# Eight groups of four feature tiles of the first layer by seven block products, with Silu gates behind the last exponential

## The chip, the cores and the metric

The kernel runs on one core of a Trainium2 chip. The metric is the device time of one execution in microseconds (us), taken as the median of several runs. TensorE (PE in the profile) multiplies matrices, PEld is its weight load, VectorE (DVE), ScalarE (ACT) and GpSimd (POOL) work on elements, and SyncE (SP) issues most transfers.

## The reference

Attention with routing by clusters, and then a two-layer network with Silu. A query sees the keys that have its cluster.

```python
q_assign = argmax(q_n @ c_n.T); k_assign = argmax(k_n @ c_n.T)      # 16 clusters a head
scores = where(q_assign == k_assign, q @ k.T / sqrt(64), -1e9)
attn = softmax(scores) @ v              # 4 batches, 8 heads, 768 tokens, 64 a head
x = attn.transpose(0, 2, 1, 3).reshape(3072, 512)
h = x @ w_in                            # 512 x 2048
out = (h * sigmoid(h)) @ w_out          # 2048 x 512
```

## The kernel before

The work is cut by batch `b` (0 to 3) and half `c` of a batch's 768 tokens (`HALF` = 384), written (b, c) below.

**Attention.** There are 192 score units: for a head, a half of the queries and two key tiles, `qk_mm` (L354) makes two matmuls of 384 columns and `exp` (L359) one exponential of 768 elements. `pv` (L371) multiplies by the values, with a column of twos for the sum of the weights, so `norm` (L381, L383) gives half of the attention output. It is transposed into `xt`, by a transfer or on TensorE (`xn_t`, L393, for the last).

**First layer.** For each of 16 feature tiles `fb` of 128, `unit_a_rows` (L421) makes four matmuls of 384 columns into a PSUM bank; what comes out is h/2. `tanh` (L441, ScalarE) and `gate` (L444, VectorE) form (tanh(h/2) + 1) * h/2, which is Silu(h), in f16 in the tile `gt`. When all scores have been issued, the two double banks of the scores (tag "st") are free, and `unit_a2` (L467, L468) takes two feature tiles at once there; the code calls these places `halls`.

**Second layer.** Single token tiles go through `part_b` (L480). Pairs of token tiles go through the class `Pair` (L561), which multiplies 2x2 blocks with seven products instead of eight. Its left operands are sums of four blocks (`sums`, L544, on VectorE). Sum 1 and 2 have tiles of their own ("sg"); sum 3 and 4 overwrite rows of `gt` that earlier products read, and so wait for these. Its right operands are sums of weights made once (`tw_piece`, L514).

**The order.** Every instruction's place in its engine's queue is chosen while the program is built, by a planner at the end of the kernel. It holds a clock and a list of ready pieces per engine, with an assumed duration for each piece (a feature tile 0.655 us on TensorE, a gate 0.52 us on VectorE), and issues what is ready, by rank. `options` lists what TensorE may do next: scores when they are due by a pace (`PACE`, `LEAST`, `GAIN`), then waiting pieces, the first layer from the queue `qa`, the second from `qb`. Four single PSUM banks (`bank`, `done`) go around between attention, first and second layer. `unit_piece` takes a feature tile from `qa`; `NU` is the number of score units, so `unit == NU` means that the last scores have been issued. `new_pair` sets up a pair and says which sum waits for what.

Tiles of staging space are reused by tag: "ab0" to "ab11" hold transposed keys and queries, "raw" and "hl" their loads.

Of the kernel before, what the change touches and what calls it, by code (L numbers as in the profile page):

```python
# [34 lines left out]
def kernel(  # L35
# [10 lines left out]
    nc = tc.nc  # L46
# [385 lines left out]
    def unit_a_end(b, c, fb, ph):  # L432
        if (b, c) not in gts:
            gts[b, c] = mp.tile([128, NFB, HALF], f16, name="gt", bufs=2)
        gt = gts[b, c]
        unit_a_rows(ph, b, c, fb, [NR - 1])

        tn = mp.tile([128, HALF], f32, name="tn", bufs=4)

        def tanh():  # L440
            nc.scalar.activation(out=tn, in_=ph[:, 0:HALF], func=AF.Tanh, bias=0.0, scale=1.0)  # L441

        def gate():
            nc.vector.scalar_tensor_tensor(out=gt[:, fb, :], in0=tn, scalar=1.0, in1=ph[:, 0:HALF], op0=ALU.add, op1=ALU.mult)  # L444
            done(ph)

        def act():
            tanh()
            gate()

        act.tanh, act.gate = tanh, gate
        return act

    def unit_a2(b, c, fb):
        if (b, c) not in gts:
            gts[b, c] = mp.tile([128, NFB, HALF], f16, name="gt", bufs=2)
# [4 lines left out]
        tn = mp.tile([128, 2, HALF], f32, name="tn2", tag=f"ab{fb // 2 % 2}", bufs=1)  # L461

        def act():
            act.tanh()
            act.gate()

        act.tanh = lambda: nc.scalar.activation(out=tn, in_=ph[:, :, 0:HALF], func=AF.Tanh, bias=0.0, scale=1.0)  # L467
        act.gate = lambda: nc.vector.scalar_tensor_tensor(  # L468
            out=gt[:, fb : fb + 2, :], in0=tn, scalar=1.0, in1=ph[:, :, 0:HALF], op0=ALU.add, op1=ALU.mult
        )  # L470
        return act
# [58 lines left out]
    class Pair:  # L530

        def __init__(self, kind, b, r1, r2, j2, sgs, last=False):
            self.last = last
            self.kind, self.b, self.j2, self.sgs, self.r1, self.r2 = kind, b, j2, sgs, r1, r2
            self.s1 = self.s2 = None

        def sums(self, k):
            if k == 1:
                self.s1, self.s2 = (mp.tile([128, HK, 128], f16, name="sg", tag=x, bufs=1) for x in self.sgs)
            s1, s2, a11, a12, a21, a22 = self.s1, self.s2, self.r1(0), self.r1(1), self.r2(0), self.r2(1)  # L540
            o, x, y, op = (
                (s1, a21, a22, ALU.add), (s2, s1, a11, ALU.subtract), (a21, a11, a21, ALU.subtract), (a12, a12, s2, ALU.subtract)
            )[k - 1]
            nc.vector.tensor_tensor(out=o, in0=x, in1=y, op=op)  # L544

        def product(self, k):
            if k == 1:
                self.A = bank("po")
                self.B = bank("po3") if self.last else self.A[:, HD:DM]
            if k == 2:  # L550
                self.Y = bank("po2")
            up = k in (3, 5)
            o = (self.Y if k == 2 else self.B if up else self.A)[:, 0:HD]
            l = self.s1 if k == 5 else self.s2 if k == 6 else self.r1(k > 1) if k < 4 else self.r2(k == 4)
            begins = (1, 2, 5) if self.last else (1, 2)
            for f in range(HK):
                if k < 4:
                    x = wout_s[:, f if k == 1 else HK + f, HD * up : HD * up + HD]
                else:
                    x = tw({4: 3, 5: 0, 6: 2, 7: 1}[k], f)[:, 0, :]  # L560
                nc.tensor.matmul(  # L561
                    o, l[:, f, :], x, start=(f == 0 and k in begins), stop=(f == HK - 1), skip_group_check=True
                )
# [39 lines left out]
        def c21_last(self):  # L603
            nc.scalar.activation(out=self.ot2[:, 0:HD], in_=self.A[:, 0:HD], func=AF.Copy, bias=0.0, scale=1.0)
            nc.scalar.dma_start(self.rows()[:, 0, :], self.ot2[:, 0:HD])

    def w_load(n, after=None):
        if after is not None:
# [259 lines left out]
    def chain(job, b):  # L868
# [23 lines left out]
        def landed(t):  # L892
            i = int(job.name[1:])
            turn_at[i] = t
            if i in after_turn:
                after_turn.pop(i)(t)
            turning(t + ROOM[b - 1])
# [138 lines left out]
    for b, c in kinds:  # L1036
# [3 lines left out]
        elif cross:  # L1040
            kinds[b, c] = ["x", 1, 2] if c else [0, 1]

    def room(key):
# [11 lines left out]
    def norm_piece(n, t):  # L1055
        b, c, i = n // 8, n // 4 % 2, n // 8 * H + 2 * (n % 4)

        def ready(t):
            nonlocal released
            if n % 4 == 3:  # L1060
                released += 1
                x_at[b, c] = t
                qa.extend((b, c, fb) for fb in range(NFB))

        def after(t):
            if by_dma(n):
# [20 lines left out]
    def new_pair(b, c, kind):  # L1087
# [3 lines left out]
        r_ = room(key)  # L1091
        if kind == "x":
            r2 = (lambda h: cps[b][h]) if b in cps else tokens(b, 0, NM - 1)
            pairs[key] = Pair(r_, b, tokens(b, 1, 0), r2, NM - 1, SG[r_])
        else:
            pairs[key] = Pair(r_, b, tokens(b, c, t + 1), tokens(b, c, t), c * NM + t, SG[r_], key == LAST)
        watch.setdefault((b, c), []).append((key, "12" if kind == "p" else "1"))
        pr = pairs[key]

# [2 lines left out]

        when(key, ("lo2", "hi2", "turn"), sum_(1, 0.0))
        when(key, ("s1", "lo1"), sum_(2, 0.0))
        when(key, ("s2", "s1", "lo1"), sum_(3, 0.5))
        when(key, ("s2", "hi1", "p2"), sum_(4, 0.5))
        if not users[r_] or "over" in at[users[r_][-1]]:
            tell(key, "turn", 0.0)
        users[r_].append(key)
        def over(t):  # L1110
# [19 lines left out]
    if 0 in CROSS:  # L1130
        kept(0, 0, 1.0)

    def unit_piece(two=False):
        b, c, fb = qa.pop(0)
        if two:
            qa.pop(0)
            halls.pop(0)
        act = (unit_a2 if two else unit_a)(b, c, fb)

        def gated(t):  # L1140
# [4 lines left out]
            for h, name in enumerate(("lo", "hi")):  # L1145
                need = [gate_at.get((b, c, x)) for x in range(h * HK, h * HK + HK)]
                if h == fb // HK and None not in need:
                    for key, rows in watch.get((b, c), ()):
                        for x in rows:
                            tell(key, name + x, max(need))  # L1150
                    if c == 0 and b in CROSS:
                        kept(b, h, t)

        def then(t):
            add("ACT", t + 0.2, 0.8 if two else 0.42, act.tanh, lambda t: add("DVE", t + 0.1, 0.92 if two else 0.52, act.gate, gated))
            if fb == 0 and kinds[b, c][0] != 0:
                for kind in kinds[b, c]:
                    if kind in ("p", "x"):
                        new_pair(b, c, kind)
                    else:  # L1160
                        qb.extend((b, c, kind, n) for n in range(4))
            elif fb == NFB - (2 if two else 1) and kinds[b, c][0] == 0:
                qb.extend((b, c, t_, n) for t_ in kinds[b, c] for n in range(4))

        return then

    def sent(t):
        clock["SP"] = max(clock["SP"], t) + 0.6
# [57 lines left out]
    def options(t):  # L1226
# [3 lines left out]
        if unit < NU and unit - 2 in exp_at and 6 * pv_next > unit - LEAD:  # L1230
            i, c, m = units[unit]
            jn = {qc[i, c][0].name, kt[i, 2 * m][0].name}
            if all(j in code_at for j in jn):
                r = max([exp_at[unit - 2]] + [code_at[j] for j in jn])

                x = unit // 24
                stock = 0.655 * len(qa) + 0.868 * len(qb) + sum(works[released:x])
                for hb in {q[:2] for q in qa}:
                    if kinds[hb][0] == 0 or hb + (0,) in qa:
# [5 lines left out]
        if unit == NU and here and halls and len(qa) > 1 and qa[0][2] % 2 == 0 and qa[0][:2] in x_at:  # L1245
# [20 lines left out]
    def tensor_piece(o):  # L1266
        nonlocal unit, pv_next, turn, scored
        rank, r, length, what = o
        if what == "qk":
            u = unit  # L1270
            unit += 1

            def then(t):
                add("ACT", t + 0.2, 0.75, lambda: exp(u), lambda t: exp_at.__setitem__(u, t), 0.2)

            run("PE", r, length, lambda: qk_mm(u), then)
            scored = max(clock["PE"] - 0.325, scored + 0.8)
# [3 lines left out]
        elif what == "pv":  # L1281
            n = pv_next
            pv_next += 1
            run("PE", r, length, lambda: pv(n // 8 * H + 2 * (n % 4), n // 4 % 2), lambda t: (pv_at.__setitem__(n, t), norm_piece(n, t), [f(t) for f in after_pv.pop(n, [])]))
        elif what in ("a", "aa") or isinstance(what, tuple):
# [21 lines left out]
    while True:  # L1307
# [14 lines left out]
        else:  # L1322
            lanes[e].remove(piece)
            run(e, piece[0], *piece[2:])
    assert not qa and not qb and not later
# [1 line left out]
_INS = ['q', 'k', 'v', 'centroids', 'moe_w_in', 'moe_w_out']  # L1327
_OUTS = [((3072, 512), 'float32')]
# [25 lines left out]
```

## Time and profile before

| | us |
|---|---|
| median of 3 runs | 300.08 |
| the runs | 297.98, 333.51, 300.08 |
| span of the profiled execution | 297.1 |
| TensorE busy | 288.0 (97% of the span) |
| VectorE busy | 219.7 (74%) |
| ScalarE busy | 221.7 (75%) |
| GpSimd busy | 72.3 (24%) |

The profile is of one execution of its own; its span goes from the first to the last instruction, and a run's time lies somewhat above a span. Rows of the groups read: line, engine, operation, output <- inputs, shapes, count | busy us, mean ns of one | idle time of the engine just before, and what ended it. Matmuls overlap in the profile, so the mean of one is its latency and not its issue rate. In the chain of waits each step goes back to what released it; a piece of the chain has a start and a length, and pieces on one engine that touch give its issue rate. A table by stretches has, for each engine, busy time and (x) instructions, then TensorE's granted clock, the share of the DMA engines and GB/s.

### The profile page before, as it was taken

The page shows a single profiled execution, that of the slowest core. Times are in us where ns is not written, and L with a number is a line of the kernel's source. Part 1 is how long each engine was busy: PE and PEld are TensorE (multiplying, and loading weights), DVE is VectorE, ACT ScalarE, POOL GpSimd, SP SyncE. Part 2 cuts the span into 40 slices and gives each one's busy share as a digit, 9 for nine tenths or more (in the row PEclk, how much of TensorE's full clock was granted, in tenths as well). Part 3 has the DMA queues.
Part 4 walks back from the last instruction along what each step waited for, and adds up shares of the span by engine and source line. Part 5 has one row for each costly group of instructions (what it writes and reads, how often), then busy time and mean ns, then how long its engine had stood idle before and what let it go on. Part 6 is the DMA issues. An engine that isn't in the chain of part 4 may idle for free.

```text
span 297.1 us, 8186 instructions
## 1 busy us (share of the span) xinstructions
PE 288.0 (97%) x3273; PEld 203.4 (68%) x3273; DVE 219.7 (74%) x459; ACT 221.7 (75%) x365; POOL 72.3 (24%) x133
## 2 busy tenths in 40 slices
PE   7899799999999999999999999999999999999995
PEld 3786666566766566667766776678767786767783
DVE  5998559586897799997797766997664553569743
ACT  5899689765896579988579668997798879845410
POOL 2889510001031023544232560243200000000000
PEclk9999999999999999999999999999999999999999
DMA  6689999999866599999877979785220020110113
GB/s 208 206 244 204 158 257 228 170 235 185 242 128 174 133 214 227 209 223 196 232 175 144 196 215 226 170 126 119 74 57 17 13 86 15 49 38 0 35 38 141
DMA packets 77220, 44.61 MB, mean 150 GB/s; under 512 B 56288, under 2 KB 73088, under 8 KB 77184
## 3 DMA queue, kind: packets, MB, share of 16 engines
q1 hardware_dynamic: 71952, 35.55, 51.7%
q0 software_dynamic: 4800, 8.13, 15.0%
q8 instruction: 25, 0.41, 0.6%
q10 hardware_dynamic: 432, 0.43, 0.4%
q14 instruction: 11, 0.09, 0.1%
HBM read 27.30 MB, written 6.29 MB: 113 GB/s over the span
## 4 chain that ended last, share of the span: by engine, by line
PE 85%; DMA 7%; POOL 2%; DVE 2%; issue 1%; ACT 1%; SPq 0%; POOLq 0%; DVEq 0%; ACTq 0%
PE ph L421 28%; PE pS L354 18%; PE po L561 16%; PE pO L371 10%; PE po L480 9%; DMA raw<-in_q_dram 3%; PE psN L180 3%; DMA ab<-cd 3%; DMA ab<-cdt 1%; POOL hl L125 1%; DVE hl L132 1%; DVE ab L166 1%; POOL vt L295 1%; POOL win_s L613 0%; PE px L393 0%
## 5 line engine op out<-in xcount | busy, mean ns | idle before, releaser
L359 ACT ACTIVATE P<-pS 128x768 f16<-128x768 f32 x192 | 156.9, 826 | 36.9 <-PE pS L354 36.0
L421 PE MATMUL ph<-xt,win_s 128*128 128x384 f16 x512 | 97.6, 326 | 0.0
L354 PE MATMUL pS<-ab 128*128 128x384 f16 x384 | 93.2, 326 | 2.2 <-DMA ab<-cd 1.5
L444 DVE SCALAR_TENSOR_TENSOR gt<-tn,ph 128x384 f16<-128x384 f32 x110 | 58.7, 550 | 21.0 <-ACT tn L441 20.4
L421 PEld LDWEIGHTS <-win_s 128*128 128x128 f16 x512 | 49.3, 98 | 31.1
L441 ACT ACTIVATE tn<-ph 128x384 f32<-128x384 f32 x110 | 55.1, 514 | 3.3 <-PE ph L421 2.4
L354 PEld LDWEIGHTS <-ab 128*128 128x128 f16 x384 | 34.5, 98 | 20.8 <-issue 2.5
L371 PEld LDWEIGHTS <-P 128*128 128x128 f16 x1152 | 39.7, 97 | 5.0 <-DVE ab L166 0.9
L371 PE MATMUL pO<-vt,P 128*128 128x65 f16 x1152 | 41.2, 193 | 0.3 <-DVE ab L166 0.3
L132 DVE SCALAR_TENSOR_TENSOR hl<-raw,hl 128x768 f16<-128x768 f32 (+3 forms) x35 | 32.8, 939 | 1.2 <-POOL hl L125 0.5
L561 PEld LDWEIGHTS <-gt 128*128 128x128 f16 x304 | 29.3, 98 | 5.9 <-DVE gt L544 0.4
L480 PE MATMUL po<-wout_s,gt 128*128 128x512 f16 x128 | 32.5, 379 | 0.0
L295 POOL CAST vt<-vn 128x384 f16<-128x384 f32 x32 | 18.8, 598 | 56.2 <-DMA vn<-in_v_dram 40.7
L561 PE MATMUL po<-wout_s,gt 128*128 128x256 f16 x192 | 24.4, 273 | 0.0
L224 POOL TENSOR_SCALAR od<-od 128x96 f16<-128x96 f16 x16 | 9.3, 580 | 53.3 <-DVE od L217 53.2
L381 DVE RECIPROCAL zr<-pO 128x6 f32<-128x6 f32 x32 | 6.2, 193 | 18.9 <-PE pO L371 18.8
L180 PEld LDWEIGHTS <-ab 128*128 128x128 f16 x458 | 17.3, 97 | 4.0 <-DVE ab L166 0.3
L480 PEld LDWEIGHTS <-gt 128*128 128x128 f16 x128 | 12.0, 98 | 10.6
L383 DVE TENSOR_TENSOR xn<-pO,zr 128x384 f16<-128x384 f32 x32 | 17.8, 557 | 1.1
L180 PE MATMUL psN<-stk,ab 128*128 128x32 f16 (+1 forms) x458 | 18.6, 188 | 0.0
L561 PE MATMUL po<-tw,sg 128*128 128x256 f16 x128 | 16.3, 273 | 0.0
L192 DVE TENSOR_REDUCE L<-psN 128x192 f32<-128x384 f32 (+1 forms) x27 | 14.8, 549 | 1.9 <-PE psN L180 1.7
(101 smaller groups left out, 259.0 us busy)
## 6 DMA issues: line engine op xcount, KB each, us to landing
raw<-in_k_dram SPq DMA_DIRECT2D x31, 192.0 KB, 4.0
out_dram<-ot SPq DMA_DIRECT2D x23, 256.0 KB, 2.4
raw<-in_q_dram SPq DMA_DIRECT2D x24, 192.0 KB, 3.9
vn<-in_v_dram SPq DMA_DIRECT2D x16, 192.0 KB, 4.2
vn<-in_v_dram POOLq DMA_DIRECT2D x16, 192.0 KB, 4.3
win_s<-in_moe_w_in_dram POOLq DMA_DIRECT2D x8, 256.0 KB, 6.2
wout_s<-in_moe_w_out_dram POOLq DMA_DIRECT2D x4, 512.0 KB, 18.8
raw<-in_q_dram SPq DMA_DIRECT2D x2, 384.0 KB, 4.2
```

Source lines behind the costliest of these rows:

```text
L132: nc.vector.scalar_tensor_tensor(out=hl[:, s, 1, :], in0=raws[job.name][:, s, :], scalar=QS, in1=hl[:, s, 0, :], op0=ALU.mult, op1=ALU.sub ...
L180: nc.tensor.matmul(L[:, n % g, :, n // g], ab[:, i, :], stk[:, job.groups[i // 3][0], x : x + w], start=(x == 0), stop=(x + w == 2 * HC),)
L295: nc.gpsimd.tensor_copy(vt[:, :, 0:D], vns.pop(i))
L354: nc.tensor.matmul(pS[:, e, 0:HALF], abs_[kj.name][:, kn, :], rhs, start=True, stop=True)
L359: nc.scalar.activation(out=P, in_=pst.pop(u)[:, :, 0:HALF], func=AF.Exp, bias=0.0, scale=ESC)
L371: nc.tensor.matmul(o[:, (2 * t + h) * VW : (2 * t + h + 1) * VW], Ps[i + h, c, j // 2][:, j % 2, ts(t, 128)], vtb[(i + h) % 13][:, j, 0:VW ...
L383: nc.vector.tensor_tensor(out=xn, in0=ov[:, :, 0:D], in1=zr.unsqueeze(2).to_broadcast([128, 2 * NM, D]), op=ALU.mult)
L421: nc.tensor.matmul(ph[:, 0:HALF], win_s[:, r, ts(fb, 128)], xts[b, c][:, r, :], start=(r == 0), stop=(r == NR - 1))
L441: nc.scalar.activation(out=tn, in_=ph[:, 0:HALF], func=AF.Tanh, bias=0.0, scale=1.0)
L444: nc.vector.scalar_tensor_tensor(out=gt[:, fb, :], in0=tn, scalar=1.0, in1=ph[:, 0:HALF], op0=ALU.add, op1=ALU.mult)
L480: nc.tensor.matmul(po, gts[b, c][:, fc, ts(t, 128)], wout_s[:, fc, :], start=(fc == 0), stop=(fc == NFB - 1))
L561: nc.tensor.matmul(o, l[:, f, :], x, start=(f == 0 and k in begins), stop=(f == HK - 1), skip_group_check=True)
```

## The change

Three things are changed.

**Groups of four feature tiles by seven block products.** Two groups of (2, 1) and three each of (3, 0) and (3, 1) are listed in `QUADS`; the other feature tiles go one by one as before, in the order of `ORDERS` (an entry from 100 on is a group). In a group the 512 inputs, the four feature tiles and the 384 tokens are each cut in two, and the seven products of a group (class `Quad`) are four matmuls of 192 columns each. The token sums (`x_sum`, 12 VectorE instructions) and the weight sums (`t_piece`, 16 instructions on VectorE or GpSimd) are formed in staging tiles. Two copies out of PSUM and four additions per group put the products together; four activations of 384 elements and their gates follow, on VectorE or, with two instructions, on GpSimd. The planner runs at most two groups at a time before the last scores, and four after that.

**Silu.** Behind the last exponential a table load for Silu is issued, and from then on first-layer results go through one Silu activation with scale 2, straight into `gt`; no gate follows.

**Own tiles.** For the last two pairs of the second layer, sums 3 and 4 have tiles of their own, and wait for no product. `tn2` moves to other tags, and from score unit 155 on the planner uses other numbers for pace and rank.

```diff
 def tanh():
+    if silu_on:
+        nc.scalar.activation(out=gt[:, fb, :], in_=ph[:, 0:HALF], func=AF.Silu, bias=0.0, scale=2.0)
+        done(ph)
+        act.gate = None
+        return
     nc.scalar.activation(out=tn, in_=ph[:, 0:HALF], func=AF.Tanh, bias=0.0, scale=1.0)
...
 def sums(self, k):
     if k == 1:
-        self.s1, self.s2 = (mp.tile([128, HK, 128], f16, name="sg", tag=x, bufs=1) for x in self.sgs)
+        self.s = [mp.tile([128, HK, 128], f16, name="sg", tag=x, bufs=1) for x in self.sgs]
+        if len(self.s) == 2:
+            self.s += [self.r2(0), self.r1(1)]
...
+QUADS = {(2, 1): (2, 3), (3, 0): (1, 2, 3), (3, 1): (1, 2, 3)}
+ORDERS = {(2, 1): [4, 0, 1, 6, 103, 3, 2, 7, 102, 5], (3, 0): [102, 103, 1, 101, 2, 3, 0], (3, 1): [0, 101, 102, 1, 3, 103, 2]}
+HT = HALF // 2
...
+def t_piece(s, r, e, v):
+    TV[0] = v
+    a, b_, op = (
+        (wblk(2 + r, 1), wblk(r, 1), ALU.subtract), (t_at_(0, r), wblk(r, 0), ALU.add),
+        (wblk(2 + r, 0), t_at_(1, r), ALU.subtract), (wblk(r, 1), wblk(r, 0), ALU.subtract),
+    )[s]
+    (nc.gpsimd if e == "P" else nc.vector).tensor_tensor(out=t_at_(s, r), in0=a, in1=b_, op=op)
...
+    a, b_, op = (
+        (a21, a22, ALU.add), (z[:, 0], a11, ALU.subtract), (a11, a21, ALU.subtract), (a12, z[:, 1], ALU.subtract),
+    )[k - 1]
+    nc.vector.tensor_tensor(out=z[:, k - 1], in0=a, in1=b_, op=op)
...
+            def gate(eng):
+                if eng == "P":
+                    nc.gpsimd.tensor_tensor(out=tn, in0=tn, in1=h, op=ALU.mult)
+                    nc.gpsimd.tensor_tensor(out=o, in0=tn, in1=h, op=ALU.add)
+                else:
+                    nc.vector.scalar_tensor_tensor(out=o, in0=tn, scalar=1.0, in1=h, op0=ALU.add, op1=ALU.mult)
...
+    def product(self, k):
...
+        o = self.Y if k in (2, 5, 3) else self.A
+        for j in range(2):
+            for r in range(2):
+                f = 4 * n + (2 if k == 3 else 0) + j
...
+                nc.tensor.matmul(
+                    o[:, HT * j : HT * j + HT], w, x,
+                    start=(k in (1, 2, 5, 3) and j == 0 and r == 0), stop=(r == 1), skip_group_check=True,
+                )
...
+    def plus(self, k):
...
+        nc.vector.tensor_tensor(
+            out=getattr(self, o).rearrange("p j t -> p (j t)"), in0=i, in1=x.rearrange("p j t -> p (j t)"), op=ALU.add
+        )
...
+OWN = {(B - 1, 1, "x"): SG["x"] + ("ab10", "ab11"), LAST: ("ab6", "ab7", "ab8", "ab9")}
...
+        if key in OWN:
+            when(key, ("s1", "lo1"), sum_(3, 0.5))
+            when(key, ("s2", "hi1"), sum_(4, 0.5))
+        else:
+            when(key, ("s2", "s1", "lo1"), sum_(3, 0.5))
+            when(key, ("s2", "hi1", "p2"), sum_(4, 0.5))
...
+        self.q, self.left, self.at, self.asked, self.hall = Quad(b, c, n, hall), [1, 2, 6, 5, 3, 7, 4], {}, set(), hall
...
+        if here and qa[0][2] >= 100:
+            r = max(x_at[qa[0][:2]], s_at.get((*qa[0][:2], 2), 1e9), t_at.get((3, 1, (qa[0][2] - 100) // 2), 1e9))
+            if len(quads) < [2, 4][unit == NU]:
...
+                def last():
+                    exp(u)
+                    if u == NU - 1:
+                        nc.scalar.preload_act_table(AF.Silu)
+                        silu_on.append(True)
...
+    def late_part():
+        nonlocal PACE, LEAST, GAIN, HOLD, SIDE, ROUND
+        PACE, LEAST, GAIN, HOLD, SIDE, ROUND = 1.47, 37, 0.085, -24, 2, 7
```

Matmuls of a group, in place of 16 of 384 columns: 28 of 192 columns, in the order of the products 1, 2, 6, 5, 3, 7, 4. Product 6 goes onto product 1's bank once that has been copied, product 5 starts the second bank again once product 2 has been added, and so on: products 6, 5, 3, 7 and 4 each wait for a copy or an addition of the same group.

More of the change, by code (lines that the diff above doesn't have):

```diff
@@ L465, in act, with tanh @@
             act.gate()
-        act.tanh = lambda: nc.scalar.activation(out=tn, in_=ph[:, :, 0:HALF], func=AF.Tanh, bias=0.0, scale=1.0)
+        def tanh():
+            if silu_on:
+                nc.scalar.activation(out=gt[:, fb : fb + 2, :], in_=ph[:, :, 0:HALF], func=AF.Silu, bias=0.0, scale=2.0)
+                act.gate = None
+                return
+            nc.scalar.activation(out=tn, in_=ph[:, :, 0:HALF], func=AF.Tanh, bias=0.0, scale=1.0)
+        act.tanh = tanh
         act.gate = lambda: nc.vector.scalar_tensor_tensor(
@@ new lines, with gating, tanh @@
+    silu_on = []
+    def gating(h, o, after):
+        def tanh():
+            if silu_on:
+                nc.scalar.activation(out=o, in_=h, func=AF.Silu, bias=0.0, scale=2.0)
+                after()
+                return
+            tn = mp.tile([128, 2, HT], f32, name="tn", bufs=4)
+            nc.scalar.activation(out=tn, in_=h, func=AF.Tanh, bias=0.0, scale=1.0)
+            def gate(eng):
[4 more added lines that the diff above has]
+                    nc.vector.scalar_tensor_tensor(out=o, in0=tn, scalar=1.0, in1=h, op0=ALU.add, op1=ALU.mult)
+                after()
+            tanh.gate = gate
+        tanh.gate = None
+        return tanh
@@ L1041, with t_step, t_start, s_step @@
             kinds[b, c] = ["x", 1, 2] if c else [0, 1]
+    quads, s_at, t_at = [], {}, {}
+    WAIT = 0.4
+    ready_t = [0]
+    def t_step(n, t, v):
+        if n < 8:
+            s, r = divmod(n, 2)
+            pool = backlog("POOL", t) + POOLT < backlog("DVE", t)
+            eng, length = ("POOL", 1.7) if pool else ("DVE", 0.4)
+            add(eng, t, length, lambda: t_piece(s, r, eng[0], v), lambda t: (t_at.__setitem__((s, r, v), t), t_step(n + 1, t, v)), 1.0)
+    def t_start(t):
+        ready_t[0] += 1
+        if ready_t[0] == B * H - H + 1 and any(n > 1 for x in QUADS.values() for n in x):
+            t_step(0, t, 1)
+    POOLT = 3.0
+    date(143, t_start)
+    if any(n < 2 for x in QUADS.values() for n in x):
+        date(182, lambda t: t_step(0, t, 0))
+    def s_step(b, c, k, t):
+        if k < 5:
+            add("DVE", t, 0.33, lambda: x_sum(b, c, k), lambda t: (s_at.__setitem__((b, c, k), t), s_step(b, c, k + 1, t)))
+    def parts(b, c):
+        if (b, c) not in QUADS:
+            return list(range(NFB))
+        return list(ORDERS[b, c])
     def room(key):
@@ L1062, in ready @@
                 x_at[b, c] = t
-                qa.extend((b, c, fb) for fb in range(NFB))
+                qa.extend((b, c, fb) for fb in parts(b, c))
+                if (b, c) in QUADS:
+                    s_step(b, c, 1, t)
         def after(t):
@@ L1144, in gated @@
             gate_at[b, c, fb] = t
[L1145 to L1152, printed above, removed]
-        def then(t):
[L1155 to L1163, printed above, removed]
@@ L1165, in unit_piece, with next_, whole @@
-        return then
+            whole(b, c, fb, t)
+        def then(t):
+            def next_(t):
+                if act.gate:
+                    add("DVE", t + 0.1, 0.92 if two else 0.52, act.gate, gated)
+                else:
+                    gated(t)
+            add("ACT", t + 0.2, 0.8 if two else 0.42, act.tanh, next_)
+            end(b, c)
+        return then
+    begun_ = set()
+    def whole(b, c, fb, t):
+        for h, name in enumerate(("lo", "hi")):
+            need = [gate_at.get((b, c, x)) for x in range(h * HK, h * HK + HK)]
+            if h == fb // HK and None not in need:
+                for key, rows in watch.get((b, c), ()):
+                    for x in rows:
+                        tell(key, name + x, max(need))
+                if c == 0 and b in CROSS:
+                    kept(b, h, t)
@@ L1167, in sent, with quad_piece, quad_step @@
+    def quad_piece(hall):
+        b, c, n = qa.pop(0)
+        if hall:
+            halls.pop(0)
+        g = Going(b, c, n - 100, hall)
+        quads.append(g)
+        then = quad_step(g)
+        return lambda t: (then(t), end(b, c))
+    def quad_step(g):
+        k = g.left.pop(0)
+        if not g.left:
+            quads.remove(g)
+        g.q.product(k)
+        return lambda t: g.tell(f"p{k}", t)
     def sent(t):
@@ L1236, in options @@
                 x = unit // 24
-                stock = 0.655 * len(qa) + 0.868 * len(qb) + sum(works[released:x])
+                stock = sum(0.655 if q[2] < 100 else 2.34 for q in qa) + 0.868 * len(qb) + sum(works[released:x])
                 for hb in {q[:2] for q in qa}:
-                    if kinds[hb][0] == 0 or hb + (0,) in qa:
+                    if kinds[hb][0] == 0 or hb not in begun_:
                         stock += work[hb] - 10.48
@@ L1284, in tensor_piece @@
             run("PE", r, length, lambda: pv(n // 8 * H + 2 * (n % 4), n // 4 % 2), lambda t: (pv_at.__setitem__(n, t), norm_piece(n, t), [f(t) for f in after_pv.pop(n, [])]))
+        elif isinstance(what, tuple) and what[0] == "q":
+            box, g = [], what[1]
+            if not isinstance(g, Going):
+                turn = (turn + 1) % ROUND
+            run("PE", r, length, lambda: box.append(quad_step(g) if isinstance(g, Going) else quad_piece(g)), lambda t: box[0](t))
+        elif isinstance(what, tuple) and what[0] == "a":
+            turn = (turn + 1) % ROUND
+            box = []
+            run("PE", r, length, lambda: box.append(unit_piece(False, what[1])), lambda t: box[0](t))
         elif what in ("a", "aa") or isinstance(what, tuple):
@@ L1324 @@
             run(e, piece[0], *piece[2:])
-    assert not qa and not qb and not later
+    assert not qa and not qb and not later and not quads
 _INS = ['q', 'k', 'v', 'centroids', 'moe_w_in', 'moe_w_out']
```

167 lines of the change are left out of this document (151 added, 16 removed).

## The prediction

> **What bounds the kernel now.** I read the span and the slices first, then the chain that ended last in the stretches that the change can touch, then the busy times by stretch, then single rows.
>
> ```profile
> span 297.1 us, 8186 instructions
> PE 288.0 (97%) x3273; PEld 203.4 (68%) x3273; DVE 219.7 (74%) x459; ACT 221.7 (75%) x365; POOL 72.3 (24%) x133
> PE   7899799999999999999999999999999999999995
> PEclk9999999999999999999999999999999999999999
> ```
>
> TensorE is busy in nearly every slice, at full granted clock. Busy time alone flatters it, because the matmul ends are modelled and overlap. So the next view is the chain, in three stretches: 200 to 230, 230 to 255, and 255 to the end.
>
> ```profile
> by line: PE ph L421 30.3%; PE po L561 29.1%; PE pS L354 24.9%; PE pO L371 13.6%; PE psN L180 2.3%
> by line: PE po L561 31.5%; PE pS L354 28.6%; PE ph L421 23.4%; PE pO L371 17.5%
> 258.87 1.10 PE pO L371 x36
> ...
> 261.88 6.50 PE ph L421 x40
> ...
> 278.38 15.04 PE po L561 x136
> 293.41 0.02 issue
> 293.43 0.38 ACT ot L604
> ```
>
> From 200 us to 293.4 us the chain stays on TensorE: nobody else is ever what the end waits for. These pieces also give issue rates free of the overlap: a product of 384 columns takes 6.50/40 = 0.1625 us, one of 256 columns 15.04/136 = 0.1106 us, one of 65 columns 1.10/36 = 0.0306 us. The change touches nothing before about 200 us (its first new work needs the last batch's loads, and (2, 1)'s transposed attention), so what it can win is TensorE time between there and 293.4 us. The 3.7 us behind the last matmul (a copy of 0.38 us and the last store) stay.
>
> The other engines in the same stretches (columns: PE, PEld, DVE, ACT, POOL):
>
> ```profile
> 200.00:215.00 15.00, 15.00 (x208) 12.17 (x205) 10.70 (x23) 11.53 (x18) 4.62 (x12) 1.00 0.45 99
> 215.00:230.00 15.00, 15.00 (x142) 10.33 (x139) 8.62 (x17) 13.14 (x25) 0.44 (x1) 1.00 0.15 37
> 230.00:245.00 15.00, 15.00 (x197) 12.03 (x195) 8.14 (x16) 11.89 (x18) 0.00 (x0) 1.00 0.17 49
> 245.00:258.00 13.00, 13.00 (x125) 8.86 (x121) 5.91 (x13) 11.95 (x22) 0.00 (x0) 1.00 0.13 37
> 258.00:270.00 12.00, 12.00 (x118) 8.73 (x116) 8.68 (x15) 5.91 (x10) 0.00 (x0) 1.00 0.07 23
> 270.00:281.00 11.00, 11.00 (x84) 7.95 (x82) 9.01 (x14) 5.10 (x8) 0.00 (x0) 1.00 0.04 13
> ```
>
> VectorE idles 4.30 + 6.38 + 6.86 + 7.09 = 24.6 us from 200 to 258 us, ScalarE 9.5 us; GpSimd is nearly free. From 258 us on ScalarE is half idle and VectorE works 17.7 of 23 us.
>
> **The change part by part.** *The products.* A group of four feature tiles is 16 matmuls of 384 columns now, 16 x 0.1625 = 2.60 us. By seven block products it is 7 x 4 = 28 matmuls of 192 columns. The trace has no 192; between its 65 and 256 columns the line gives 0.0306 + 127/191 x 0.0800 = 0.0838 us, so 28 x 0.0838 = 2.35 us. Bounds: half of a 384 (0.0813, 2.28 us) and a weight load that cannot hide:
>
> ```profile
> L421 PEld LDWEIGHTS <-win_s 128*128 128x128 f16 x512 | 49.3, 98 | 31.1
> ```
>
> At 98 ns each, 28 loads would take 2.74 us and the group would lose 0.14 us. I take 0.0838, because the 65-column products issue every 0.0306 us with a fresh 128x128 weight each, so loads do overlap. Eight groups: 8 x (2.60 - 2.35) = **2.0 us saved**.
>
> The Trainium skill (TensorE: Matmul & The Clock Gate, section "Wait — 56ns, not 53.3ns?") gives a warm product N/2.4 GHz plus a fixed 2.5 ns. Its 384 (162.5 ns) is the trace's; its 192 would be 82.5 ns, and the eight groups would save 2.3 us.
>
> *What the groups add elsewhere.* Per group two copies out of PSUM, four VectorE additions with a PSUM operand, all 128x384, and the same four activations and gates as now.
>
> ```profile
> L441 ACT ACTIVATE tn<-ph 128x384 f32<-128x384 f32 x110 | 55.1, 514 | 3.3 <-PE ph L421 2.4
> L444 DVE SCALAR_TENSOR_TENSOR gt<-tn,ph 128x384 f16<-128x384 f32 x110 | 58.7, 550 | 21.0 <-ACT tn L441 20.4
> L594 DVE TENSOR_TENSOR ot<-po,uu 128x512 f32<-128x512 f32 x7 | 4.8, 689 | 3.1 <-PE po L561 3.0
> L587 DVE TENSOR_TENSOR ot<-po,uu 128x256 f32<-128x256 f32 x8 | 3.4, 422 | 6.4 <-PE po L561 4.8 <-ACT ot L567 1.7
> L514 DVE TENSOR_TENSOR tw<-wout_s,tw 128x512 f16<-128x512 f16 (+1 forms) x5 | 2.5, 524 | 0.0
> L404 DVE COPY xt<-px 128x384 f16<-128x384 f16 x8 | 2.7, 354 | 3.4 <-PE px L393 3.4
> L295 POOL CAST vt<-vn 128x384 f16<-128x384 f32 x32 | 18.8, 598 | 56.2 <-DMA vn<-in_v_dram 40.7 <-PE ph L421 11.1 <-PE pO L371 4.3
> L125 POOL TENSOR_SCALAR hl<-raw 128x576 f16<-128x576 f32 (+1 forms) x6 | 11.1, 1852 | 6.0 <-DMA raw<-in_q_dram 4.6 <-PE pTq L155 1.3
> ```
>
> An addition of 384 lies midway between 422 and 689, so 0.555 us; a copy 0.51 us. Five groups ((2, 1) and (3, 0)) come mostly before the last exponential: VectorE gains 5 x (4 x 0.555 + 0.5) = 13.6 us there. The token sums are 12 instructions of 384 f16 elements (between 0.354 and 0.524, say 0.4): 4.8 us. The weight sums are 16 of 512 f16: 8.4 us, if none goes to GpSimd. Together 27 us against the 24.6 us that VectorE has free: it would be full, but for what GpSimd takes. There a 384 operation has no row of its kind: 0.60 us (the cast) to 1.23 us (1852 x 384/576), and a gate needs two. I count this at nothing for TensorE, because sums and gates have due times far ahead (weight sums begin about 205 us, are read later) and TensorE has other ready work, the block products of the second layer; without that cover it is the rival below. No DMA is added or moved past a queue.
>
> *Silu behind the last exponential.* Now the last exponential is the ACT row at 256.50, and these follow:
>
> ```profile
> 256.50 0.84 ACT L359 ACTIVATE P<-pS 128x768 f16<-128x768 f32 x1
> 257.19 0.92 ACT L441 ACTIVATE tn<-ph 128x384 f32<-128x384 f32 x2
> 258.91 0.81 ACT L467 ACTIVATE tn<-ph 128x768 f32<-128x768 f32 x1 [0.80 <-PE ph L421]
> 261.92 0.49 ACT L402 ACTIVATE xt<-px 128x384 f16<-128x384 f16 x1 [2.20 <-PE px L393]
> L647 ACT ACT_TABLE_LOAD x1 | 1.3, 1283 | 1.7 <-PEq L1338 1.7
> L468 DVE SCALAR_TENSOR_TENSOR gt<-tn,ph 128x768 f16<-128x768 f32 x9 | 8.6, 952 | 3.5 <-ACT tn L467 3.4
> ```
>
> A table load of 1.28 us goes in behind the exponential; queued behind it are the copies and activations of the running units, and the PSUM banks that these hold. ScalarE then idles 0.80 and 2.20 us, so it catches up by 262 us; TensorE meanwhile has the attention product, two block products and the transposes (1.10 + 1.75 + 0.17 us). Cost nothing, at most 1.28 us. The Trainium skill (ScalarE: Activation LUTs, "What ACT_TABLE_LOAD costs") adds a drain of about 1.38 us to a load of 1.28 us: the load is the trace's, no run here shows the drain in mid-stream; with it at most 2.66 us.
>
> Silu itself has no row; a Tanh of the same shape takes 0.51 us, and I take that (bounds: 0.42 and 0.95, the PSUM reads of 256 and of 768 elements on VectorE). It removes VectorE's gates there: nine of 0.95 us and the short ones. Off the path, they pay for the groups' additions in the tail (three groups, 6.7 us).
>
> *Own tiles for the last two pairs' sums.* Sums 3 and 4 need no longer wait for products that read the rows they overwrite. What this is worth stands in the last 10 us:
>
> ```profile
> 284.32 1.04 PE L561 MATMUL po<-tw,gt 128*128 128x256 f16 x8
> 285.20 1.04 PE L561 MATMUL po<-tw,sg 128*128 128x256 f16 x8
> ...
> 287.82 1.04 PE L561 MATMUL po<-tw,sg 128*128 128x256 f16 x8
> 288.76 2.52 PEld L561 LDWEIGHTS <-gt 128*128 128x128 f16 x24 [0.19 <-DVE gt L544]
> 288.77 1.92 PE L561 MATMUL po<-wout_s,gt 128*128 128x256 f16 x16
> ```
>
> A block product takes 0.88 us from start to start; the one at 287.82 is followed after 0.95 us, since the next waited for the sum. A second wait of 0.19 us stands 2.7 us later. Some 0.07 us each: **0.15 us saved**.
>
> *Group chains.* A group is a chain: product 1, copy, addition, product 5, copy, addition, product 7, addition, product 4: 4 x 0.335 + 2 x 0.51 + 3 x 0.555 = 4.0 us, with 2.35 us of TensorE work in all. Alone it would leave TensorE idle for 1.7 us; two side by side, or other work, cover it. The bound is 0 to 8 x 1.7 = 13.6 us; I take 0.1 us each, **0.8 us lost**, near the lower end, because the second layer's block products already have such chains and the chain view shows no TensorE wait after 200 us.
>
> Sum: -2.0 - 0.15 + 0.8 = -1.4 us; span 297.1 to 295.7 us. The runs shown lie 0.9 us (fastest, 297.98) and 3.0 us (median, 300.08) above that span; I add 1.4 us, nearer to the fastest, which gives **297.1 us**. Against the median shown that is 1% less; about 2% is what a measurement here can tell from no change.
>
> **The rivals.**
> *Groups starve TensorE (slower).* Two PSUM banks are held per group from its first product to its last addition, and before the last scores two groups may hold all four. If VectorE is as full as reckoned, each addition queues behind others. It decides at 0.27 us of idle per group (2.15/8): from there the change loses. At 0.5 us each the span is 297.1 - 2.15 + 4 = 299.0 and the time about 300.4; at 1 us each 303 and 304.4. For it: 27 us of work against 24.6. Against: GpSimd idle, and a clean chain today. Chance 0.24, of which 0.09 beyond 2%.
>
> *The table load reaches TensorE.* All four banks wait for ScalarE at 257 us, and 1.28 us is lost: span 297.0, time 298.4. Against it stand the idle 3.0 us behind it. Chance 0.08. The drain of the Trainium skill's page, named above, would make it 2.66 us: span 298.4, time 299.8.
>
> *Narrow products do not issue faster (the saving is not there).* At 98 ns a load, the span is 297.1 + 8 x 0.14 + 0.65 = 298.9, time 300.3. The 65-column rate speaks against it. Chance 0.03.
>
> *VectorE and GpSimd slow each other.* In the two stretches before and after 220 us the same sum takes:
>
> ```profile
> L544 DVE TENSOR_TENSOR sg<-gt x3: 682/777/993, 132.3 to 201.5; 128x1024 f16<-128x1024 f16 x3
> L544 DVE TENSOR_TENSOR sg<-gt x4: 683/689/692, 235.6 to 280.7; 128x1024 f16<-128x1024 f16 x4
> ```
>
> GpSimd works in the first stretch and not in the second; 777 against 689 is 13% on the 13 us of SBUF sums, 1.7 us of VectorE. If all reached TensorE: span 297.4, time 298.8. Chance 0.05. The Trainium skill (GPSIMD Engine Reference, "Key points") says that GpSimd shares its SBUF interfaces with VectorE and contends with instructions of two SBUF inputs; the first row agrees.
>
> *More than the products.* The pace and order of the last part are changed too, and the runs' offset is uncertain. Beyond 2% below the median shown (under 294.1) the span must fall by 3.9 us at the smallest offset. TensorE's chain has no such slack. Chance 0.08.
>
> **How the numbers follow.** Forecast 0.52, its own range 295.6 (2.3 us saved, no idle, offset 0.9) to 298.7 (offset 3.0). The 80% range takes in half of the starving cases and the small tail below: 294.6 to 301.2. Faster by over 2%: 0.08; slower: 0.09; within: 0.83.
>
> **What would show it.** Right: 128 fewer wide and 224 more narrow products at 0.083 to 0.084 us, the chain still all TensorE after 200 us, the last matmul about 1.4 us earlier, one more table load of 1283 ns. Wrong: TensorE waits for additions or copies of the groups, windows of 215 to 258 us below full PE, or VectorE near 100% there.

## The result and the profile after

| | before | after |
|---|---|---|
| median | 299.52 us (13 runs) | 297.30 us (13 runs) |
| time against before | | 0.9947, 95% interval 0.9921 to 0.9972 |
| span of the profiled execution | 297.1 us | 295.2 us |

The change makes the kernel 0.5% faster; the prediction was 297.1 us. A run far above the others of its kernel is left out of the ratio: here one of each, and such runs of the kernels below.

The page of the changed kernel begins:

```profile
span 295.2 us, 8473 instructions
PE 286.7 (97%) x3369; PEld 209.9 (71%) x3369; DVE 234.2 (79%) x509; ACT 228.2 (77%) x385; POOL 73.2 (25%) x133
```

TensorE has 96 more instructions: 8 x (28 - 16). The chain of waits of the changed kernel, in its stretches 200 to 230 and 230 to 255, and then pieces from there to the end:

```profile
by line: PE po L574 27.3%; PE pS L354 27.1%; PE ph L421 17.3%; PE pO L371 14.2%; PE ph L715 6.6%; PE py L715 5.5%; PE psN L180 2.3%
by line: PE po L574 34.1%; PE pS L354 26.6%; PE pO L371 17.5%; PE ph L715 10.2%; PE py L715 6.6%; PE ph L421 5.2%; issue 0.1%
...
240.70 0.48 PE pS L354 x2
...
261.61 0.23 PE px L393 x3
261.84 1.30 PE ph L421 x8
263.14 1.80 PE ph L715 x20
...
266.25 0.99 PE ph L715 x12
...
281.02 10.49 PE po L574 x96
291.51 0.02 issue
291.54 0.38 ACT ot L617
```

Line 715 is the groups' products, 574 the pairs of the second layer. The chain still never leaves TensorE. Twelve narrow products take 0.99 us, so one takes 0.0825 us. Where pieces are longer than that, TensorE waited: 20 products in 1.80 us are 0.15 us too long, the transposes took 0.23 in place of 0.17 us, and around the scores at 240.70 lie 0.19 us. These 0.40 us are all its idle time behind 200 us by the starts of its products. Only the 0.15 us are a wait for a group's addition; the transposes waited for the attention output, and the scores for ScalarE.

To leave out the first 200 us, where both kernels wait for loads by turns, I measure from a common point: the first scores of batch 3, ahead of which TensorE's queue is the same in all kernels here. These are TensorE's rows in time in the kernel before and in the changed one:

```profile
198.21 0.49 PE L354 MATMUL pS<-ab 128*128 128x384 f16 x2
```

```profile
198.40 0.49 PE L354 MATMUL pS<-ab 128*128 128x384 f16 x2
```

From there to the copy behind the last matmul are 293.43 - 198.21 = 95.22 us before and 291.54 - 198.40 = 93.14 us after: **2.08 us less**. The products account for it: 8 x (16 x 0.1625 - 28 x 0.0825) = 2.32 us, less 0.40 us of idle, plus the 0.15 us of idle that the kernel before had. The span fell by only 1.9 us because the start was 0.19 us later.

### The profile page after: what moved, and what is told of

It is laid out like the page before. It is cut to its first block, busy times and chain, and to the rows that moved or that the text cites. A ratio compares the mean times of both kernels' runs of the same rounds, so it can differ in the third digit from the quotient of the medians.

```text
span 295.2 us, 8473 instructions
## 1 busy us (share of the span) xinstructions
PE 286.7 (97%) x3369; PEld 209.9 (71%) x3369; DVE 234.2 (79%) x509; ACT 228.2 (77%) x385; POOL 73.2 (25%) x133
## 4 chain that ended last, share of the span: by engine, by line
PE 81%; DMA 10%; ACT 5%; issue 1%; DVE 1%; SPq 1%; ACTq 0%
PE ph L421 21%; PE pS L354 18%; PE po L574 15%; PE pO L371 10%; PE po L492 8%; PE ph L715 5%; ACT P L359 3%; DMA ab<-cdt 3%; PE psN L180 2%; DMA ab<-cd 2%; DMA ab<-hl 2%; PE py L715 2%; DMA raw<-in_k_dram 1%; DMA raw<-in_q_dram 1%; DVE hl L132 1%
## 5 line engine op out<-in xcount | busy, mean ns | idle before, releaser
L421 PE MATMUL ph<-xt,win_s 128*128 128x384 f16 x384 | 75.2, 326 | 0.0
L449 DVE SCALAR_TENSOR_TENSOR gt<-tn,ph 128x384 f16<-128x384 f32 x90 | 48.0, 550 | 12.4 <-ACT tn L446 11.8
L421 PEld LDWEIGHTS <-win_s 128*128 128x128 f16 x384 | 36.6, 98 | 22.5
L446 ACT ACTIVATE tn<-ph 128x384 f32<-128x384 f32 x90 | 45.2, 514 | 3.0 <-PE ph L421 2.5
L295 POOL CAST vt<-vn 128x384 f16<-128x384 f32 x32 | 19.5, 619 | 54.9 <-DMA vn<-in_v_dram 51.9
L132 DVE SCALAR_TENSOR_TENSOR hl<-raw,hl 128x768 f16<-128x768 f32 (+3 forms) x35 | 31.6, 905 | 1.4 <-POOL hl L125 0.5
L574 PEld LDWEIGHTS <-gt 128*128 128x128 f16 x272 | 26.3, 98 | 4.8
L574 PE MATMUL po<-wout_s,gt 128*128 128x256 f16 x176 | 22.8, 272 | 0.0
L492 PEld LDWEIGHTS <-gt 128*128 128x128 f16 x128 | 12.0, 98 | 10.6
L574 PE MATMUL po<-tw,sg 128*128 128x256 f16 x144 | 18.3, 273 | 0.0
L574 PEld LDWEIGHTS <-sg 128*128 128x128 f16 x160 | 15.5, 98 | 2.3
```

The source lines that it names most:

```text
L132: nc.vector.scalar_tensor_tensor(out=hl[:, s, 1, :], in0=raws[job.name][:, s, :], scalar=QS, in1=hl[:, s, 0, :], op0=ALU.mult, op1=ALU.sub ...
L295: nc.gpsimd.tensor_copy(vt[:, :, 0:D], vns.pop(i))
L421: nc.tensor.matmul(ph[:, 0:HALF], win_s[:, r, ts(fb, 128)], xts[b, c][:, r, :], start=(r == 0), stop=(r == NR - 1))
L492: nc.tensor.matmul(po, gts[b, c][:, fc, ts(t, 128)], wout_s[:, fc, :], start=(fc == 0), stop=(fc == NFB - 1))
L574: nc.tensor.matmul(o, l[:, f, :], x, start=(f == 0 and k in begins), stop=(f == HK - 1), skip_group_check=True)
```

## The experiments

The last column is the length from the common point to the copy behind the last matmul, against before's 95.22 us. It is to resolve what the times, with intervals of some 0.3%, don't. Each length is of one execution. That it resolves so much rests on this: the kernel before and the one with Silu alone, whose products and waits on TensorE are the same, agree to 0.01 us, and the other lengths come out of the products and the gaps between their starts. The length with the old pace is of a second run of that kernel.

| kernel | median us | ratio to before, 95% | length, us |
|---|---|---|---|
| Silu alone | 299.25 | 0.9985 (0.9956 to 1.0013) | 0.0 |
| all but the groups | 298.76 | 0.9976 (0.9948 to 1.0005) | -0.2 |
| five groups | 298.40 | 0.9959 (0.9928 to 0.9991) | -1.4 |
| **eight groups (the change)** | 297.30 | 0.9947 (0.9921 to 0.9972) | **-2.1** |
| nine groups | 300.00 | 1.0025 (0.9996 to 1.0055) | +0.8 |
| ten groups | 300.78 | 1.0051 (1.0024 to 1.0079) | +1.1 |
| eight, without own tiles | 299.30 (one run) | | -0.8 |
| eight, old pace | 300.11 | 1.0020 (0.9982 to 1.0058) | +1.2 |
| eight, Tanh and gates | 309.63 | 1.0365 (1.0323 to 1.0408) | +10.6 |
| eight, Tanh, no own tiles, old pace | 311.80 | 1.0412 (1.0347 to 1.0477) | +12.3 |
| eight, one at a time | 311.20 | 1.0405 (1.0365 to 1.0446) | +12.3 |

**All but the groups.** My theory was TensorE's narrower products; the rival, that Silu and the new pace bring the gain.

```diff
-QUADS = {(2, 1): (2, 3), (3, 0): (1, 2, 3), (3, 1): (1, 2, 3)}
+QUADS = {}
```

> All 16 feature tiles of every half one by one, with Silu, own tiles and the new pace numbers kept. If the gain is TensorE's narrower products (8 x 0.29 us, less about 0.25 us of new idle), the span goes back by 2.1 us, to about 297.2, and the time to about 299.4. If the gain came from Silu and the new pace, span and time stay within 0.4 us of those of the changed kernel (295.2 and 297.3).

Its common point and the copy behind its last matmul:

```profile
197.91 0.49 PE L354 MATMUL pS<-ab 128*128 128x384 f16 x2
292.96 0.38 ACT ot L617
```

1.9 of the 2.1 us go back, as the theory has it. The span falls short of the expectation (296.6 for 297.2 us), since the common point was 0.49 us earlier than in the changed kernel, and so does the median (298.76 for 299.4 us). In time alone the groups would not be proven: the medians, from different series, differ by 1.5 us, the ratios by 0.3%, and their intervals overlap. What is left, 0.2 us, is mostly the two waits of 0.08 us that the own tiles take away; TensorE has no idle step behind 200 us here.

**Silu alone.**

```diff
-QUADS = {(2, 1): (2, 3), (3, 0): (1, 2, 3), (3, 1): (1, 2, 3)}
+QUADS = {}
-    OWN = {(B - 1, 1, "x"): SG["x"] + ("ab10", "ab11"), LAST: ("ab6", "ab7", "ab8", "ab9")}
+    OWN = {}
-        PACE, LEAST, GAIN, HOLD, SIDE, ROUND = 1.47, 37, 0.085, -24, 2, 7
+        pass
```

> Silu behind the last exponential as the one change; no groups, sums in place, old pace. If VectorE was hidden in the tail before, taking 25 gates from it moves nothing: span within 0.4 us of that of before, the table load included. If the load reaches TensorE it is 1.3 us slower; if the gates held the tail back, it is over 0.5 us faster.

Nothing moves. Busy time from 258 to 281 us, of the kernel before and of this one:

```profile
258.00:281.00 23.00, 23.00 (x199) 16.68 (x197) 17.69 (x28) 11.00 (x18) 0.00 (x0) 1.00 0.06 19
```

```profile
258.00:281.00 23.00, 23.00 (x199) 16.71 (x197) 7.64 (x14) 11.66 (x17) 0.00 (x0) 1.00 0.06 19
```

The third pair of numbers is VectorE: 10 us of gates are gone, and TensorE does not notice. The table load in ScalarE's rows:

```profile
256.47 0.84 ACT L359 ACTIVATE P<-pS 128x768 f16<-128x768 f32 x1
257.33 1.28 ACT L1563 ACT_TABLE_LOAD   x1
258.62 0.87 ACT L442 ACTIVATE gt<-ph 128x384 f16<-128x384 f32 x2
259.38 0.82 ACT L474 ACTIVATE gt<-ph 128x768 f16<-128x768 f32 x1
263.02 0.81 ACT L474 ACTIVATE gt<-ph 128x768 f16<-128x768 f32 x1 [2.82 <-PE ph L421]
```

From the last exponential's end to the first Silu lie 1.31 us, and later ScalarE waits 2.82 us for TensorE: the load is hidden, with room to spare.

**Eight groups with Tanh and gates.**

```diff
-                        nc.scalar.preload_act_table(AF.Silu)
-                        silu_on.append(True)
+                        pass
...
-                add("ACT", t + 0.2, 0.75 + (2.0 if u == NU - 1 else 0.0), last, lambda t: exp_at.__setitem__(u, t), 0.2)
+                add("ACT", t + 0.2, 0.75, last, lambda t: exp_at.__setitem__(u, t), 0.2)
...
-        tn = None if silu_on else mp.tile([128, 2, HALF], f32, name="tn2", tag=f"ab{2 + fb // 2 % 2}", bufs=1)
+        tn = None if silu_on else mp.tile([128, 2, HALF], f32, name="tn2", tag="tnx", bufs=2)
```

> Tanh and gates to the end, no second table load; groups, own tiles and pace kept (the Tanh results of double tiles get places of their own). VectorE has 4.6 us free between 258 and 281 us, and 25 gates of 0.55 us are 13.7 us. If Silu is what pays for the groups, VectorE is full there, TensorE waits for it, and the span grows by 1 to 5 us, but for gates that GpSimd takes. If VectorE has room enough in other places, the span stays within 0.4 us of 295.2.

The cost, 12.7 us against the change, is more than the 1 to 5 us expected. TensorE's greatest wait (us in all, times, longest), and then the stretches behind 270 us:

```profile
PE ph L715 <- DVE hq L738: 5.7, 3, 2.9
```

```profile
270.00:281.00 11.00, 6.95 (x57) 5.69 (x55) 8.25 (x19) 5.40 (x13) 3.17 (x4) 0.81 0.01 2
281.00:294.00 13.00, 9.71 (x68) 7.71 (x66) 11.38 (x19) 4.52 (x11) 3.54 (x3) 0.76 0.00 0
```

L738 is the groups' additions. They queue behind gates on VectorE (11.4 of 13 us), some gates go to GpSimd at 1 us per instruction and two instructions each, and TensorE idles up to 2.9 us at a time. The number behind the five engines is TensorE's granted clock: 0.81 and 0.76. By their starts, products of 192 columns then issue every 0.16 us in place of 0.0825, and 3.7 of the 12.7 us are lost to that. The gates on GpSimd also held VectorE back: of its sums of 1024 elements, two that ran beside such a gate took 1.48 and 1.49 us, where the others of that stretch took 0.68 to 0.69. So Silu alone is worth 0.0 us, and under the groups 12.7 us. That is its worth in this order: the lists and the pace were chosen for the kernel with Silu, and no other order was tried without it.

**One group at a time.**

```diff
-            if len(quads) < [2, 4][unit == NU]:
+            if len(quads) < 1:
```

> At most one group at a time, before and after the last scores. A group's chain is 4.0 us long with 2.3 us of TensorE work. If other work covers the rest, TensorE's idle time after 200 us stays under 0.5 us and the span within 0.4 us of 295.2. If a group needs another group beside it, each of eight leaves up to 1.7 us idle, mostly in the three of (3, 1) where little else is left: 2 to 6 us more.

TensorE's greatest wait in it:

```profile
PE ph L715 <- DVE hq L738: 6.4, 9, 1.1
```

and the stretch from 294 us on:

```profile
294.00:310.00 16.00, 11.64 (x84) 9.29 (x83) 7.63 (x15) 2.63 (x6) 0.00 (x0) 0.79 0.19 67
```

This is the chain of a group laid bare: nine waits for an addition. The cost is 14.4 us against the change. By the starts of the products, 9.7 us of TensorE's idle time lie at the groups' own additions and copies, 1.2 us per group and below the prediction's bound of 1.7; 2.3 us are lost to slow products at the lower clock, and the rest are waits elsewhere, such as those of second-layer products for their copies. Groups need groups beside them.

**Five, nine and ten groups.**

```diff
-QUADS = {(2, 1): (2, 3), (3, 0): (1, 2, 3), (3, 1): (1, 2, 3)}
+QUADS = {(2, 1): (2, 3), (3, 0): (1, 2, 3)}                                # five
+QUADS = {(2, 1): (2, 3), (3, 0): (0, 1, 2, 3), (3, 1): (1, 2, 3)}          # nine; (3, 0): [102, 103, 101, 100]
+QUADS = {(2, 1): (2, 3), (3, 0): (0, 1, 2, 3), (3, 1): (0, 1, 2, 3)}       # ten; also (3, 1): [101, 102, 100, 103]
```

> Groups in (2, 1) and (3, 0) only, five; (3, 1) by single feature tiles and double tiles; Silu, own tiles and new pace kept. If each group is worth its columns wherever it stands, 5 x 0.29 = 1.45 us come of the 1.9 that the eight gave over none, last matmul 0.5 us later than with eight. If most of TensorE's new idle (0.2 us of the 0.4 behind 200 us lie behind 258 us) is due to the three groups of (3, 1), it is 0.3 us later.

> (3, 0) wholly by groups (four), (3, 1) as in the changed kernel (three). With ten groups TensorE idled 4.2 us behind 200 us. If the limit is (3, 1), whose groups have the least other work beside them, nine groups idle little and save 0.3 us more than eight. If the single feature tiles of (3, 0) were what covered the chains, it idles 2 us or more and is slower than eight by that much.

> Batch 3 wholly by groups: four groups in (3, 0) and four in (3, 1), ten in all. If columns decide, TensorE saves another 2 x 0.29 = 0.58 us, span about 294.6 and time about 296.7. If the groups' chains and VectorE are at their limit already, the new groups leave TensorE idle by more than 0.29 us each, the last matmul is no earlier, and waits of TensorE for VectorE appear behind 258 us.

Five give 1.2 us over none: 5 x 0.29 = 1.45 less 0.25 us of idle. The three groups of (3, 1) give another 0.7. The ninth costs 2.8 us. Pieces of its chain:

```profile
256.94 0.69 DVE ot L607
257.63 0.48 DVE hq L738
...
267.68 1.03 DVE hq L738 x2
...
270.43 1.02 PE po L574 x8
271.48 0.38 ACT ot L580
271.86 0.45 ACT gt L662
```

VectorE and ScalarE now stand in the chain. The ninth group replaces the four single tiles of (3, 0), and TensorE's idle time grows from 0.4 to 3.6 us, 3.0 of it behind 258 us. This fits the second expectation: the single tiles were the work that covered the other chains. It is not shown to be the only cause, since nine groups were run in one order alone, with no other place for the ninth. The tenth costs another 0.4 us.

**Without own tiles, and with the old pace.**

```diff
-    OWN = {(B - 1, 1, "x"): SG["x"] + ("ab10", "ab11"), LAST: ("ab6", "ab7", "ab8", "ab9")}
+    OWN = {}
```

> Sums 3 and 4 of the last two pairs overwrite their operands again, as before; all else as changed. By the prediction's step TensorE waits twice for the sums in the last 13 us, 0.07 us each, and the last matmul is 0.15 us later against a common point at 200 us. If the own tiles matter more with groups in front of them, because the sums begin later, it is 0.5 us or more.

The second answer: 1.3 us, where without groups the own tiles and the new pace together are worth 0.2 us. Its chain at the end:

```profile
278.98 0.02 issue
279.00 0.56 DVE hq L738
279.56 0.34 DVE ot L600
279.90 0.04 issue
279.94 1.03 PE po L574 x8
...
281.31 7.00 PE po L574 x64
288.31 0.02 issue
288.33 0.70 DVE gt L557
289.04 0.05 issue
289.08 4.64 PE po L574 x40
```

TensorE stands still while a sum is formed over rows that product 2 has just read. By the starts of the products, 0.95 us are lost there, 0.27 us ahead of it, where an output's addition (L600) is queued behind a group's, and 0.08 us at a later sum: together the 1.3 us. That the wait for a sum is longer with groups in front (0.95 us, against 0.08 before) is shown; why the order left nothing to put there is not.

```diff
-        PACE, LEAST, GAIN, HOLD, SIDE, ROUND = 1.47, 37, 0.085, -24, 2, 7
+        pass
```

> Groups, Silu and own tiles with the old numbers for pace and rank to the end. If the groups need the earlier scores and the larger stock of second-layer work that the new numbers leave, TensorE idles behind 230 us for 1 us or more and the gain is gone (299 us and up). If the order was free anyway, time and span stay within 0.4 us of 297.3 and 295.2.

> The old pace numbers again, for the trace alone, since the trace of the timed run shows the clock at 0.56 throughout. Its time was 2 to 3 us above that of the changed kernel. If the stock of second-layer work at the last exponential is what the new numbers buy, TensorE waits for additions behind 255 us, 2 us or more in all; if the cause is ScalarE or the scores, the idle lies between 215 and 255 us.

The old numbers cost 3.3 us. TensorE's waits behind 200 us, in the second run's trace:

```profile
PE ph L715 <- DVE hq L738: 0.7, 1, 0.7
PE pO L371 <- DVE gt L449: 0.5, 1, 0.5
PE pO L371 <- DVE ot L583: 0.4, 1, 0.4
PE pS L354 <- ACT P L359: 0.2, 1, 0.2
```

Neither expectation holds alone: by the starts of its products, 1.7 us of TensorE's idle lie between 215 and 255 us and 2.0 behind. Waits of the attention product for a gate or an output's addition are waits for a PSUM bank, and that of the scores is for ScalarE. Which of the six numbers matters was not tried.

**All edits but the groups undone.**

> Eight groups with Tanh and gates to the end, pair sums in place, old pace. If the groups' saving stands by itself, the span is about 295.4. If Silu carries their additions, TensorE waits for VectorE behind 258 us as without Silu alone, and the time is 308 us or more.

The edits are those of the three kernels above together. It lands at 12.3 us over before, and Silu is the greatest part of that. The prices are not a sum: one by one the three edits cost 12.7, 1.3 and 3.3 us, together 14.4.

## Why the prediction was right, and where its terms were off

The mechanism was right: TensorE sets the time behind 200 us, and the change is worth the columns that it saves there, less a little idle. The sizes:

- *Products.* 2.0 us forecast, 2.32 measured. The line from 65 to 256 columns gave 0.0838 us; it is 0.0825. Its upper end was read too high: the piece of 136 products in 15.04 us held both waits for sums, and the changed kernel's last piece, 96 products in 10.49 us, gives 0.1093. From there the line gives 0.0829; what is left was not followed up. The Trainium skill's N/2.4 GHz + 2.5 ns (TensorE: Matmul & The Clock Gate, "Wait — 56ns, not 53.3ns?") gave 82.5 ns, and the trace agrees (0.0825 us). That narrow products might not issue faster is excluded.
- *Group chains.* 0.8 us forecast, 0.40 measured, and only 0.15 of that at a group's addition. The danger was real: with one group at a time it is 9.7 us of the bound's 13.6. The reason given for the low end, that the second layer has such chains without a wait, was not enough; the cover came from groups side by side, Silu, own tiles and pace together.
- *Own tiles.* 0.15 us forecast from before's two waits; all but the groups gives 0.2, with the pace in it. But under the groups they are worth 1.3 us: the term was read from the old tail, and the groups change what waits there.
- *Pace.* The prediction gave it no term. It is worth 3.3 us to the groups.
- *Silu.* "Off the path, they pay for the groups' additions" was right, and the price of a missing cover was not worked out: 12.7 us. These rows of the changed kernel's groups show what was to be hidden:

```profile
L738 DVE TENSOR_TENSOR hq<-ph,hq 128x384 f32<-128x384 f32 x22 | 11.7, 553 | 2.2 <-PE ph L715 1.4 <-ACT gt L662 0.7
L643 DVE TENSOR_TENSOR ts<-win_s 128x512 f16<-128x512 f16 x8 | 3.2, 425 | 0.0
L655 DVE TENSOR_TENSOR xs<-xt 128x384 f16<-128x384 f16 x6 | 2.1, 352 | 0.2 <-ACT xt L402 0.2
L1563 ACT ACT_TABLE_LOAD x1 | 1.3, 1283 | 0.0
```

Additions came as reckoned (0.555, 0.553). The sums were cheaper: 0.352 for 0.4 and 0.425 for 0.524 us.

- *VectorE full before the last exponential.* It did not come to that. The changed kernel by stretches:

```profile
200.00:215.00 15.00, 15.00 (x185) 11.61 (x182) 13.42 (x34) 12.57 (x22) 4.85 (x11) 1.00 0.43 95
215.00:230.00 15.00, 15.00 (x184) 12.24 (x182) 11.21 (x25) 13.40 (x24) 0.55 (x1) 1.00 0.16 41
230.00:245.00 15.00, 14.97 (x209) 12.51 (x208) 12.30 (x29) 12.99 (x22) 0.00 (x0) 1.00 0.17 49
245.00:258.00 13.00, 13.00 (x146) 11.01 (x144) 10.75 (x26) 11.60 (x19) 0.00 (x0) 1.00 0.13 37
```

VectorE works 47.7 of 58 us (before, 33.4): 14.3 us more, not 27. By the starts of its instructions, 14 of the groups' additions lie ahead of 258 us, not 20, and 8 of the 12 token sums; ScalarE took 10 of the 16 copies. GpSimd, which I thought would help, took no gate and no sum (133 instructions, as before); it was not needed.

- *The table load.* Hidden, as forecast. The drain that the Trainium skill adds to it (ScalarE: Activation LUTs, "What ACT_TABLE_LOAD costs") is not seen: 0.01 us lie between the load's end and the first Silu in the run with Silu alone.
- *From span to time.* I added 1.4 us. The profiled run has 297.3 us at a span of 295.2, so it is 2.1. The span came out 0.5 us below the forecast and this 0.7 above, so part of the close hit is two misses that cancel. There is luck in the base too: the 1% forecast was against a median of three runs, 300.08 us; over 13 runs it is 299.52, and the ratio says 0.5%.

The starving rival did not come true at eight groups, but it decides where the change stops: its point was 0.27 us of idle per group; the ninth adds more than that tenfold. The rival that VectorE and GpSimd slow each other had no room here, as GpSimd works 0.55 us behind 215 us; it shows in the kernel with Tanh and gates above. By length, no version here beats the changed kernel; by time, five groups can't be told from eight.

## What to carry to other kernels

When one engine is full to the end, price an edit by the work that it takes from that engine, and then ask of every other engine whether the edit's new chains still have cover. Parts that are worth nothing alone (an activation that frees VectorE, tiles that end an overwrite, another order) can be the condition on which the paying part pays, so undo them one by one in the changed kernel, not only try them alone in the old one. Measure small effects from a common point in the trace: two kernels with the same work on TensorE agreed to 0.01 us in length, where times scatter by 1 us and more.

## What the runs showed of the hardware

TensorE's granted clock fell to half behind waits. Waits are taken here from the starts of the products. Without Silu the clock was 0.50 from 278 to 282 us, after waits of 2.6 and 0.7 us, and again from 288 to 290 us, after one of 3.1 us. With one group at a time it went down at 294.5 us and was 0.50 from 296 to 300 us, after three waits of 0.8 to 0.9 us within about 3 us; single waits near 265 us, 1.3 us there and 1.5 us with all edits but the groups undone, left it at 1.00. The Trainium skill (TensorE: Matmul & The Clock Gate, "Part 1: The HAM clock gate") says that the clock is halved after at least one idle window of about 3.4 us; the halving agrees, but no wait ahead of it was that long here.

A VectorE sum of two SBUF tiles, 1024 elements each, took 1.40 to 1.49 us beside a gate on GpSimd (five of six such in the two kernels with Tanh) and 0.68 to 0.69 us without GpSimd at work.

The Silu activation costs what Tanh does: 0.81 us for 768 elements out of PSUM, for both.
